# Seven products for eight: Strassen's scheme in the down product of an RWKV-7 and MLP kernel

## The chip, the cores and the metric

The kernel runs on one core of a Trainium2 chip. The metric is the time of one execution in microseconds on the device. All data is 32-bit floating point on the chip. TensorE, which multiplies matrices, works beside VectorE, ScalarE and GpSimd, each with its own queue of instructions; SyncE (SP) issues the transfers.

## The reference

An RWKV-7 recurrence over 768 steps (4 batches, 8 heads, head size 40), and on its output an MLP with a quick GELU:

```
for t in range(S):
    y[:, :, t] = einsum('bhd,bhde->bhe', r_t, state)
    Sa = einsum('bhde,bhe->bhd', state, a_t)
    state = state * w_t[:, :, None, :] - einsum('bhd,bhe->bhde', Sa, b_t) + einsum('bhd,bhe->bhde', v_t, k_t)
x = y.transpose(0, 2, 1, 3).reshape(3072, 320)
h = x @ w_in                              # 320 -> 2048
g = h * (1 / (1 + exp(-1.702 * h)))
out = g @ w_out                           # 2048 -> 320
```

## The kernel before

The sequence is cut into 12 chunks of 64 steps. A unit is one chunk of two batches (24 units); one step of a unit's algebra works on all its 16 heads. For each unit: decays (`decay`, `logarithm`), scaled keys and scores (`prep`), the inverse of a triangular matrix by five doubling levels (`inverse`), and the solution with the state carried over (`solve`). A level is a TensorE step (`ps_level`), a copy W, a subtraction E (line 763), a transpose ES (line 712) and a spreading EX (lines 717 and 719, on ScalarE, GpSimd or VectorE); the next level waits for EX.

When both units of chunk c are done, their outputs x go to DRAM and come back transposed into `xT_all` (three slots). Then `mlp(c)` runs on 256 tokens: `up`, 4 quarters q of 10 TensorE steps each (`ps_up`), each quarter followed by the activation `gelu(q)` into `g`; and `down(p)` for each unit p, 8 steps of 8 matmuls (`ps_down`), accumulated in the two PSUM banks of a pair, then a copy of one bank to `ob` (line 1027), an addition of the other (line 1029) and two transfers out. The last `down` is split into two halves of 160 columns.

All matmuls use the array as four tiles of 64x64: `QUARTERS` lists the four (row half, column half) pairs, and four matmuls run side by side. A 32-bit matmul is issued as two load-and-multiply pairs, so a down step of 8 matmuls is 16 instructions and a `down` is 128. Every matmul goes through the helper `mm` (line 301), so in the profile all have the line L301 and are told apart by their tiles.

The program is a list of tasks. `Plan.add` registers each with what it reads and writes; `ORDER`, written out by hand into the file, gives the sequence of all tasks, the engine of each and, for tasks with PSUM, one of four pairs of banks. Each engine runs its tasks in that sequence. The weights come as 64-bit numbers and are turned into 32-bit ones in eight pieces, the last operation of each on GpSimd (line 473).

Of the kernel before, what the change touches and what calls it, by code (L numbers as in the profile page):

```python
# [58 lines left out]
class Plan:  # L59
# [5 lines left out]
    def add(self, rank, engines, fn, reads=(), uses=(), writes=(), room=(), pair=None, most=None, size=0, release=0.0):  # L65

        t = Task(rank, engines, fn, pair, most, size)
        t.release = release  # L70
# [39 lines left out]
0s 8s 1s4 5s 102a 7s 6s 3a 9s 157a 87p0 88p1 10s 89a1 100p2 90a0 95d 13s4 4a 11s 93d 12s 101d2 98p3 2s 94d 97d 17s 103p1 16s 96d  # L110
142p0 15s 104a1 105d1 141p2 143a0 106d 99d3 107p1 144a2 18s4 148g 132p3 108a1 109d1 155p0 45s4 149d 27s 150g 156d0 158p2 14s4
110p1 159a2 160d2 91s4 130p0 161d 19a 24s4 112d1 162p2 111a1 22d 26s4 25s 163a2 113p1 20d 131a0 152g 164d2 34s4 92a 272s 21d
165p0 114a1 151g 271s 147a 153p2 115d1 273s 166a0 167d0 116p1 23g 28a 154d2 262p0 343s 117d1 263p2 133a3 342s 264a2 118d1 168p3
36s 31d 33s 119p1 276g 169a3 170d3 35s 120d1 42s 122a1 171p2 277d 278g 121a 43s 124d1 123a1 126p3 173d2 125a1 127d3 285a 29d
128p1 172a2 44s4 286p3 30d 54s4 37a 174p2 129d1 32g 51s4 288d3 134p1 178a2 146s4 175d2 145s 265a0 135d1 176a 187p0 289d 136p1
275s4 179a2 266g 61s 38d 138d1 188a0 341s 139s 287a3 181p0 39d 185p3 40d 137a1 177a2 290p1 313d 180a2 182a0 53s4 280g 279g 274s
186a3 183p2 292d1 281p0 291a1 333p3 41g 184d2 332p1 282d0 189p2 334a3 60s4 345s 314p0 190d2 316a0 346d 355a 191p3 347d 315d0
193d3 356p2 344s2 62s 140s 194s 195s4 192d3 293p0 335a1 358d2 46a 283p3 359d 317p1 294a0 295d0 349g 318a1 284d3 360p0 269a 348d
350g 296p1 336d 361a0 362d0 319p3 383d 357a2 297a1 298d1 384p0 321p2 49d 320a3 299p1 385a0 47d 322a2 63s4 363p3 300a1 301d1
323d2 386a0 302p1 364a3 365d3 353p0 351p2 306a1 48d 267s3 207p3 52s3 307a1 305d1 208p3 50g 268s3 64a 303d1 209p3 352d2 210p3  # L120
211p3 354d0 308a1 196p2 304a 212p3 65d 197p2 213p3 72s3 214p3 70s3 270d 55a 309p1 337s3 198p2 69s4 366p0 310a1 66d 199p2 367a0
200p2 58d 468p1 201p2 368d0 469a 473s 202p2 476s 203p2 67d 387p0 477s 470a1 490d 204p2 68g 480s 339a 205p2 369p1 388d0 206a2
215p3 371d1 218p0 219p0 56d 472s4 216p3 483g 71s4 220p0 217a3 471d 81s4 221p0 482d 79s 311p2 222p0 370a1 223p0 224p0 312d2 225p0
340d 372p3 229p1 478s4 376a3 230p1 57d 378a3 324p2 560s4 377a3 59g 226p0 78s4 375a3 325d2 231p1 73a 232p1 227p0 373d3 326p2 374d
228a0 389p3 484g 479s3 327d2 338s4 240p0 529d 390a3 481g 328d2 379p3 233p1 380a3 329d 234p1 391p2 485g 241p0 556s4 392d2 80s4
242p0 393d2 74d 486p3 235p1 487d3 530p2 236p1 75d 531a2 381p3 237p1 532a2 330s4 382d3 238p1 76d 491p2 394p3 494a2 493d2 77g
239a1 243p0 395d3 82a 488p1 557s3 396p3 489d1 474a 558s4 83d 331s 251p1 492d2 495d 252p1 84d 85d 253p1 398d3 86g 559s4 548p2
244p0 703s 397d3 549a 570d 553s 245p0 496d 550a2 552s 399d 497a 254p1 551g 554a 498p3 564d 400s 568p2 565g 499a3 246p0 569d2
500d3 563g 247p0 562d 694p2 561g 255p1 248a0 401s2 249d0 475d 256p1 250s 533p3 257p1 534a3 555d 695a 571p0 535p3 573d0 258p1
574a0 698s4 501d 696a2 609d 502g 536a3 537p2 572d0 259a1 576d 566p3 538a2 702s 402p0 575g 567d3 577a 403p0 404p0 539d2 785s3  # L130
700a 405p0 706s 708d 406p0 578p3 407p0 580d3 408p0 260d1 610p2 409p0 581d 709g 410p0 611d2 411p0 612d2 503p1 707d 582g 412a0
424p2 425p2 504d1 704s2 426p2 505d1 427p2 697d 428p2 579d3 613p1 701d 429p2 614a1 583p0 430p2 584a0 506d 431p2 585d0 432p2 507a
782s2 586d 433p2 587d 446p3 434a2 508p1 588p0 509a1 447p3 590d0 589a0 510d1 261s2 413p2 511d 699s 414p2 591d 512a 783s 415p2
592g 416p2 513p0 417p2 514a0 515d0 593p1 516d 418p2 594a1 595d1 419p2 596d 420p2 517a 597d 421p2 422p2 518p0 423a2 435p1 519d0
436p1 521d0 520g 437p1 522d0 438p1 523d0 439p1 440p1 524d0 525p2 716p0 526a2 441p1 717d0 927s 442p1 718d0 527p2 443p1 719d0
444p1 528d2 598p0 721d 445a1 540p2 720d 722g 601d0 603a0 617p1 602d0 541d2 448p3 618a1 604d0 542p2 619d1 599d0 600d 615p1 705s
544d2 449p3 616a1 781s 710d 545g 711d 605p0 723p1 606a0 450p3 607p0 451p3 546s 608d0 930s 452p3 725d1 724d1 620p0 726d 543d2
727a 773p1 453p3 621d0 778s 774a 547s 754d 728p2 622p0 454d3 455d3 729d2 456s 457p3 775a1 776g 730d2 784s 786g 779a 777s 624d0
458p3 623d0 625g 731d 793p1 833d 732a 459p3 733p2 789g 460p3 626s 734a2 794d1 735d2 714p0 790g 736d 461p3 780d 737g 1009s 918p1
755p2 923s 462p3 715d0 756a2 627s 757a2 788d 463p3 738p0 787d 464p3 739a0 740d0 919a 795p2 465d3 758p0 1006s 466d3 798a2 921d  # L140
650p3 467s 759d0 920a1 651p3 924a 928s 796d2 712p1 797d2 652p3 922s 800d 799g 653p3 932d 801a 654p3 834p0 655p3 713d1 656p3
657p3 835d0 760p2 836d0 925d 658p3 761a2 659p3 762p1 660a3 741d 628p0 742d 926s 629p0 630p0 763d1 802p2 764d1 631p0 803a2 804d2
632p0 805d 633p0 806a 743p3 634p0 746d3 635p0 747d3 837p1 931g 748d3 636p0 838a1 1007s 749d3 637p0 807p2 744d3 933g 638a0 639p1
808d2 640p1 791p3 745a 809d2 672p0 810d 792d3 811a 750p2 641p1 751a2 812p3 642p1 813a3 814d3 752p2 643p1 753d2 644p1 815d 645p1
816a 765p3 839p2 766d3 646p1 840a2 647p1 817p3 648p1 818a3 819d3 767p2 820d 649a1 821d 673p0 769d2 929s 768d2 770g 822p3 934d
674p0 825a3 826a3 940p1 827a3 675p0 1151s 828a3 935d 943a1 771s 661p2 823d3 662p2 941d1 1154s 824a 663p2 942d1 997p3 945d 944g
664p2 998a 1002s 978d 938p1 946g 665p2 939d1 666p2 772s 667p2 668p2 829p1 669p2 999a3 1000d 1001s 830d1 670p2 1003a 1011d 676p0
671a2 1004d 831p3 841p1 677p0 832d3 1005s 842d1 936p3 843d1 678p0 937d3 844p2 679p0 845d2 947p1 1010g 680d0 846p3 948a1 681d0
1012d 682s 683p2 847d3 1013g 1008s 848d3 1019p0 1014g 949d1 684p2 1022a0 1230s 849d 1233s 979p3 685p2 980a3 950d 850s 1020d0
981a3 951g 1142p1 1021d0 686p2 1024d 1143a 1147s 1023d 1025g 982p3 1057d 687p2 1152s 952p0 851s 983a3 1145g 688p2 1156d 1146s  # L150
953a0 954d0 984p3 1144a1 955d 1148a 689p2 956d 985a3 1149d 986p0 690p2 987a0 1150s 988d0 957p1 691a2 863p3 958a1 692d2 864p3
959d1 865p3 693s 960d 866p3 961d 1026p0 867p3 1027a0 1028d0 868p3 1029d 1155g 869p3 1157d 1030a 1058p2 870p3 871p3 1059a2 872p3
1060d2 1031p1 873a3 852p0 1033d1 853p0 1034d 854p0 1035d 1061p2 855p0 1062d2 1032a1 856p0 962p3 857p0 963a3 964d3 1036p1 965d
# [96 lines left out]
def rwkv7_gelu_quick(ctx: ExitStack, tc: tile.TileContext, time_d, v_d, w_d, wc_d, ak_d, b_d, rv_d, w_in, w_out, out):  # L250
    nc = tc.nc
# [735 lines left out]
    def mlp(c):  # L987
# [16 lines left out]
        def down(p):  # L1004
# [28 lines left out]
            for n, cols in enumerate([slice(0, DM // 2), slice(DM // 2, DM)] if last else [slice(0, DM)]):  # L1033
                for m in range(NM):
                    part(m, n, cols)
# [7 lines left out]
        for p in BITS:  # L1043
            down(p)
# [105 lines left out]
```

## Time and profile before

| | |
|---|---|
| median of 3 runs | 677.33 us (675.91 to 678.18) |
| profiled execution, span from the first to the last instruction | 677.7 us |
| profiled execution, time of its own | not listed beside the span |
| TensorE matmuls busy | 649.6 us, 19616 instructions |
| TensorE weight loads busy | 568.7 us, 19616 instructions |
| VectorE, ScalarE, GpSimd busy | 449.7, 329.1, 175.7 us |

The page of the profile gives busy times, the chain of work that ended last, and groups of instructions: line, engine, operation, output and inputs, shape, count, then busy time in us and the mean of one in ns, then the idle time of the engine ahead of them and what ended it. A row of the chain view is: start in us, length in us, what, and how many instructions were recorded (a few per cent of matmul records can be missing).

### The profile page before, as it was taken

Reading aid. Unit: us, or ns where it says so; the run is one execution under the profiler, and the core shown is the slowest. Engines: PE = TensorE matmul, PEld = TensorE weight load, DVE = VectorE, ACT = ScalarE, POOL = GpSimd, SP = SyncE. Lnnn points to the kernel's source line nnn. Section 1 sums busy time; section 2 is a strip of 40 time slices with the busy share of each in tenths; the row PEclk is TensorE's granted clock in tenths of the full one; section 3 lists DMA queues with packets and bytes.
Section 4 is the critical chain, followed back from the end, with each engine's and each line's share of the span. In section 5 each row is a group of like instructions: output and inputs, shape, how many; then the busy total and the mean of one; then the engine's idle time right before and its main releaser. Section 6 shows DMA issues by size and latency. Waiting matters only on the chain.

```text
span 677.7 us, 42447 instructions
## 1 busy us (share of the span) xinstructions
PE 649.6 (96%) x19616; PEld 568.7 (84%) x19616; DVE 449.7 (66%) x916; ACT 329.1 (49%) x681; POOL 175.7 (26%) x201
## 2 busy tenths in 40 slices
PE   5777999999999999999999999999999999999997
PEld 4667787787999997888888899999889798799896
DVE  5777779777867668757776687868656766675001
ACT  3676745634564655654545445455344454263010
POOL 6541443324123123123113211322411421300000
PEclk9979999999999999999999999999999999999999
DMA  6875753415324314432404513513412411200200
GB/s 208 295 255 160 226 172 97 129 42 152 107 64 131 94 58 124 114 107 65 124 14 131 149 35 108 155 33 107 140 38 62 130 53 45 69 15 14 60 13 21
DMA packets 35473, 69.74 MB, mean 103 GB/s; under 512 B 5472, under 2 KB 14816, under 8 KB 35296
## 3 DMA queue, kind: packets, MB, share of 16 engines
q1 hardware_dynamic: 35216, 66.99, 32.9%
q8 instruction: 154, 2.52, 1.6%
q14 instruction: 23, 0.19, 0.1%
q10 hardware_dynamic: 80, 0.04, 0.0%
HBM read 59.15 MB, written 7.86 MB: 99 GB/s over the span
## 4 chain that ended last, share of the span: by engine, by line
PE 88%; DMA 6%; DVE 2%; issue 1%; SPq 1%; ACT 1%; DVEq 0%; ACTq 0%
PE ps_up L301 31%; PE ps_down L301 29%; PE ps_level L301 8%; PE ps_y L301 5%; PE ps_B L301 4%; PE ps_X L301 2%; PE ps_N L301 2%; PE ps_rz L301 1%; PE ps_RV L301 1%; PE ps_A L301 1%; PE ps_zT L301 1%; SPq L331 1%; DMA w_sb<-in_w_in 1%; PE ps_cum L301 1%; PE ps_T L301 1%
## 5 line engine op out<-in xcount | busy, mean ns | idle before, releaser
L301 PE MATMUL ps_up<-xT_all,w_sb 64*64 64x256 f32 x3840 | 253.3, 377 | 2.1 <-issue 1.3
L301 PE MATMUL ps_down<-w_sb,g 64*64 64x320 f32 (+1 forms) x3200 | 241.5, 419 | 0.2 <-ACT zr L879 0.2
L301 PEld LDWEIGHTS ps_up<-xT_all,w_sb 64*64 64x64 f32 x3840 | 170.8, 133 | 18.8 <-issue 2.1
L301 PEld LDWEIGHTS ps_down<-w_sb,g 64*64 64x64 f32 x3200 | 142.5, 133 | 31.6 <-issue 0.4
L1000 ACT ACTIVATE g<-ps_up 128x1024 f32<-128x1024 f32 x48 | 49.2, 1025 | 46.3 <-PE ps_up L301 45.8
L719 POOL TENSOR_TENSOR EX<-ES,quads 128x512 f32<-128x512 f32 x30 | 39.7, 1324 | 116.4 <-DVE ES L712 77.7
L761 ACT COPY W<-ps_level 128x512 f32<-128x512 f32 x56 | 32.8, 585 | 67.7 <-PE ps_level L301 66.0
L301 PEld LDWEIGHTS ps_level<-W,EX 64*64 64x64 f32 x2560 | 60.0, 134 | 5.4 <-DVE T L840 0.2
L763 DVE TENSOR_TENSOR E<-two,ps_level 128x256 f32<-128x256 f32 x80 | 33.1, 415 | 36.5 <-ACT W L761 32.3
L301 PE MATMUL ps_level<-W,EX 64*64 64x64 f32 (+1 forms) x2560 | 56.8, 217 | 0.0
L717 ACT ACTIVATE EX<-ES,quads 128x256 f32<-128x256 f32 x82 | 37.2, 501 | 31.9 <-DVE ES L712 31.3
L629 POOL TENSOR_TENSOR ak<-ak,FT 128x512 f32<-128x512 f32 x17 | 23.0, 1353 | 77.2 <-DMA ak<-in_ak 54.4
L301 PEld LDWEIGHTS ps_level<-PT,EX 64*64 64x64 f32 x1280 | 30.7, 138 | 11.5 <-DVE EX L733 3.3
L301 PE MATMUL ps_level<-PT,EX 64*64 64x64 f32 (+2 forms) x1280 | 32.5, 234 | 6.9 <-DVE EX L733 5.0
L712 DVE STREAM_TRANSPOSE ES<-E 128x256 f32<-128x256 f32 x80 | 35.3, 443 | 4.4
L301 PE MATMUL ps_y<-RV,kh 64*64 64x104 f32 (+1 forms) x768 | 35.4, 247 | 0.9 <-DVE M L917 0.9
L301 PE MATMUL ps_y<-M,bh 64*64 64x104 f32 (+1 forms) x768 | 35.5, 247 | 0.7 <-DVE M L917 0.5
L901 ACT COPY B<-ps_B 128x416 f32<-128x416 f32 (+1 forms) x35 | 17.2, 493 | 34.4 <-PE ps_B L301 34.2
L301 PEld LDWEIGHTS ps_y<-RV,kh 64*64 64x64 f32 x768 | 29.6, 133 | 3.2 <-DVE M L917 1.5
L917 DVE TENSOR_TENSOR M<-ps_X,later 128x832 f32<-128x832 f32 (+1 forms) x24 | 23.9, 995 | 10.2 <-PE ps_X L301 10.0
L301 PE MATMUL ps_B<-RV,A 64*64 64x104 f32 (+1 forms) x768 | 29.2, 252 | 0.8 <-issue 0.8
L637 POOL TENSOR_TENSOR kh<-time,G 128x320 f32<-128x320 f32 x18 | 16.2, 901 | 51.2 <-PE ps_y L301 34.6
(133 smaller groups left out, 1099.0 us busy)
## 6 DMA issues: line engine op xcount, KB each, us to landing
ak<-in_ak SPq DMA_DIRECT2D x48, 160.0 KB
rv<-in_rv SPq DMA_DIRECT2D x48, 160.0 KB
time<-in_time SPq DMA_DIRECT2D x24, 320.0 KB
xT_all<-x_dram SPq DMA_DIRECT2D x48, 160.0 KB
wc<-in_wc SPq DMA_DIRECT2D x20, 264.0 KB
logw<-in_w SPq DMA_DIRECT2D x24, 160.0 KB
RV<-in_v SPq DMA_DIRECT2D x24, 160.0 KB
b<-in_b SPq DMA_DIRECT2D x48, 80.0 KB
```

The source lines that it names most:

```text
L301: nc.tensor.matmul(o, lhsT, rhs, start=start, stop=True, skip_group_check=True)
L331: begun.append(queue.dma_start(dst, src).ins)
L629: plan.add(R, {"DVE": 690.0, "POOL": 1270.0, "sbuf": True}, lambda t: of(t.engine).tensor_mul(ahT(), ahT(), FT_of(i)), reads=T("ak", "FT") ...
L637: plan.add(R + 4, {"POOL": 870.0, "DVE": 490.0, "sbuf": True}, lambda t, n=n, dst=dst: of(t.engine).tensor_mul(dst(i)[:, :, :D], by_head(t ...
L712: plan.add(rank, dve(256), lambda t: nc.vector.transpose(ES(n), source(t)), writes=[key("ES", n, 6)], **reads)
L717: nc.scalar.activation(dst[:, :, h], ES(n), ACT.Copy, scale=quads[:, h, :1])
L719: of(t.engine).tensor_mul(dst, ES(n).unsqueeze(2).to_broadcast([128, 8, 2, 32]), quads.unsqueeze(1).to_broadcast([128, 8, 2, 32]))
L761: plan.add(rank, any2(512), lambda t: copy(t.engine)(tiles_of(W(n + 1)), blocks(psum(t, ""), 64)), writes=[key("W", n + 1, 5)], pair=pair)
L763: plan.add(rank, dve(256), lambda t: nc.vector.tensor_sub(tiles_of(E(n + 1)), every(two32, [128, 2, 4, 32]), blocks(psum(t, ""), 64)[:, :, ...
L901: plan.add(R, any2(4 * wide), lambda t: copy(t.engine)(dst(), some(psum(t, "")[:, :, :208])), writes=[("Bv", i)] if x and c > 0 else T("B" ...
L917: plan.add(R + 1, dve(8 * wide), lambda t: nc.vector.tensor_tensor(M_of(i)[:, :, :wide].rearrange("p (j b) n -> p b j n", b=2), some(psum( ...
L1000: plan.add(-45, {"ACT": 1030.0, "table": "gelu"}, lambda t: nc.scalar.activation(g_of(c * NQ + q).rearrange("p m r n -> p r m n"), psum(t, ...
```

## The change

Chunk 0 keeps the down product as it was. For chunks 1 to 11 both units are multiplied at once: the 256 tokens are two row halves p of 128, the 2048 inner columns are split in halves by m (each quarter q holds a part of both), and the 320 output columns in two halves of 160. This gives blocks a11, a12, a21, a22 of g and B(0,0) to B(1,1) of `w_out`, and seven block products in place of eight. Each product has 4 steps (one per q) of two matmuls with 128 rows, 128 columns of weights and 160 moving columns, on the whole array: 4 pairs of load and multiply a step.

Before each step's product come the sums S1 = a21 + a22, S3 = a11 - a21, S2 = S1 - a11 and S4 = a12 - S2, one 128x256 operation per q on VectorE or GpSimd (`combined`). Four sums of weight blocks are made once (`weight_sums`), into the space in which raw weights had lain. S1 lies in the third slot of `xT_all` (so two remain for x), S2 in a block of `w_out` that is not needed any more.

Products 1, 6, 7, 4 add up in bank 0 of a pair and 2, 5, 3 in bank 1; seven evictions of 160 columns (`taken`) take the values out at the right time, four copies and three additions.

`ORDER` is new: 3043 tasks in place of 2709. The steps up to the first down step of chunk 0 stand as before.

```diff
-    def add(self, ..., release=0.0):
+    def add(self, ..., release=0.0, loose=False, bank=None):
...
-            t.after.update(o for o in writers if "PE" in o.engines)
+            if not loose:
+                t.after.update(o for o in writers if "PE" in o.engines)
...
-    plan = Plan(dict(... wz=2, ... xT=3, g=4, ob=1), 4)
+    plan = Plan(dict(... wz=3, ... xT=2, g=4, sb=1, S1=4, S2=4), 4)
...
-    wz_of = lambda i: buf("wz", i, [128, 8])
+    wz_of = lambda i: wch_of(i)[:, 0]
...
-    xT_of = lambda c: xT_all[:, c % 3].rearrange("p (q k n) -> p q k n", q=2, n=128)
+    xT_of = lambda c: xT_all[:, c % 2].rearrange("p (q k n) -> p q k n", q=2, n=128)
...
+    def weight_sums():
+        made = [(0, B(0, 1), B(0, 0), []), (1, B(1, 1), sums[:, 0], [("sum", 0)]), (2, B(1, 1), B(0, 1), []), (3, B(1, 0), sums[:, 1], [("sum", 1)])]
+        for k, x, y, after in made:
+            plan.add(60, {"DVE": 1490.0, "POOL": 2890.0, "sbuf": True}, lambda t, k=k, x=x, y=y: of(t.engine).tensor_tensor(
+                out=sums[:, k], in0=x, in1=y, op=ALU.subtract), ...)
...
+        def fast():
...
+            for q in range(NQ):
+                n = c * NQ + q
+                a11, a12, a21, a22 = (lambda n, p=p, m=m: block(n, p, m) for p, m in product(BITS, BITS))
+                combined(q, S1_of, a21, a22, ALU.add, [("weight", raws.index("x"))], [("S1", n)])
+                combined(q, a21, a11, a21, ALU.subtract, [("S1", n)], [("S3", n)])
+                combined(q, S2_of, S1_of, a11, ALU.subtract, [("S1", n), ("sum", 0), ("sum", 2)] + none, [("S2", n)])
+
+            def times(name, bank, slot, left, right, reads, kept=True):
+                for q in range(NQ):
+                    n = c * NQ + q
+
+                    def go(t, n=n, q=q):
+                        ps, a = psum(t, "ps_fast"), left(n)
+                        for f in BITS:
+                            fresh = (t.pair, bank) not in begun_banks
+                            begun_banks.add((t.pair, bank))
+                            mm(ps[:, bank, slot * HD:(slot + 1) * HD], a[:, f], right[:, q, f], fresh)
...
+            times("1", 0, 0, lambda n: block(n, 0, 0), B(0, 0), ...)
+            taken("c1", 0, 0, 0, 0, ["P1"])
+            times("2", 1, 0, lambda n: block(n, 0, 1), B(1, 0), ...)
+            taken("C11", 0, 0, 1, 0, ["P2", "c1"], True)
+            for q in range(NQ):
...
+                combined(q, a12, a12, S2_of, ALU.subtract, [("S2", n), ("P2", (c, q))], [("S4", n)])
+            times("6", 0, 0, S2_of, sums[:, 1], ..., False)
+            taken("u2", 0, 1, 0, 0, ["P6"])
+            times("5", 1, 1, S1_of, sums[:, 0], ..., False)
+            taken("d", 1, 1, 1, 1, ["P5"])
+            times("7", 0, 0, lambda n: block(n, 1, 0), sums[:, 2], ...)
+            taken("C22", 1, 1, 0, 0, ["P7", "d"], True)
+            times("3", 1, 1, lambda n: block(n, 0, 1), B(1, 1), ...)
+            taken("C12", 0, 1, 1, 1, ["P3", "u2"], True)
+            times("4", 0, 0, lambda n: block(n, 1, 1), sums[:, 3], ...)
+            taken("C21", 1, 0, 0, 0, ["P4"])
...
+        if c < FAST:
+            for p in BITS:
+                plain(p)
+        else:
+            fast()
```

`FAST` is 1. `plain(p)` is the old `down(p)` without the split of the last.

More of the change, by code (lines that the diff above doesn't have):

```diff
@@ L63, in __init__, with add @@
         self.tasks, self.made, self.used, self.of_pair = [], {}, {}, {}
-    def add(self, rank, engines, fn, reads=(), uses=(), writes=(), room=(), pair=None, most=None, size=0, release=0.0):
+    def add(self, rank, engines, fn, reads=(), uses=(), writes=(), room=(), pair=None, most=None, size=0, release=0.0, loose=False, bank=None):
         t = Task(rank, engines, fn, pair, most, size)
+        t.half = bank
         t.release = release
@@ L114 @@
[L114 to L117, printed above, removed]
@@ L246 @@
+2994d 2998g 2989a3 2991d 2999d 2995d 3022p0 3001g 3005p0 3007p0 3004p0 2797s 3024p0 3010p0 3000d 3013g 3006a0 2992g 3018p0
+3017p0 3019p0 3016p0 3020a0 3023p0 3021p0 3029p0 3027p0 3026p0 3028p0 3025a0 3030d0 3009p0 3032p0 3037p0 3015d 3014d 3011d0
+3036p0 3038p0 3012g 3039p0 3034p0 3040a0 3042s 3033p0 3031p0 3035d0 3041s
 """
@@ L267, in rwkv7_gelu_quick @@
     PARTS = 4
+    FAST = 1
     ROUNDS, WINDOW, SHARE = 4, 5000.0, 1.0
@@ L279, in rwkv7_gelu_quick @@
     banks = ctx.enter_context(tc.tile_pool(name="banks", bufs=1, space=bass.MemoryType.PSUM))
-    plan = Plan(dict(logw=3, wc=3, G=1, wch=3, wz=2, time=2, ak=2, b=2, rv=2, FT=3, GT=1, kh=2, bh=2, zr=2, rz=2,
-                     A=1, B=1, RV=2, E0=2, W0=2, P21=2, PT=2, W=2, E=2, ES=2, EX=2, T=2, Tc=1, QT=1, zraw=2, zT=1, M=2, x=1, xT=3, g=4, ob=1), 4)
+    plan = Plan(dict(logw=3, wc=3, G=1, wch=3, wz=3, time=2, ak=2, b=2, rv=2, FT=3, GT=1, kh=2, bh=2, zr=2, rz=2,
+                     A=1, B=1, RV=2, E0=2, W0=2, P21=2, PT=2, W=2, E=2, ES=2, EX=2, T=2, Tc=1, QT=1, zraw=2, zT=1, M=2, x=1, xT=2, g=4, sb=1, S1=4, S2=4), 4)
     tiles, psums, drams = {}, {}, {}
@@ L309, in pe, with pe_whole @@
         return {"PE": sum(n * 2 * max(m[0] / 1.2 + 5 if m else 58.0, cols / 1.2 + 3) for n, cols, *m in sets), "instr": sum(16 * n for n, *_ in sets)}
-    def pe_wide(*sets):
-        return {"PE": sum(n * 2 * (cols / 1.2 + 3) for n, cols in sets), "instr": sum(8 * n for n, _ in sets), "mode": 1}
+    def pe_whole(n, cols):
+        return {"PE": n * 2 * (2 * cols / 2.4 + 3), "instr": 4 * n, "mode": 1}
     def dve(n):
@@ L325, in copy @@
         return nc.scalar.copy if e == "ACT" else nc.vector.tensor_copy
-    begun = []
+    begun, begun_banks = [], set()
     def transfer(t, dst, src, queue=nc.sync):
@@ L364, in select @@
                                 pattern=[[sign, t.shape[-1]]], channel_multiplier=-sign)
-    edges = single("edges", [128, 65])
+    border = single("border", [128, 169])
+    edges = border[:, :65]
     nc.gpsimd.memset(edges, 1.0)
@@ L385, in rwkv7_gelu_quick @@
         select(within[32 * q:32 * q + 32, q % 2], ALU.is_gt, 0, -1, 0.0)
-    upper, later = single("upper", [128, 64]), single("later", [128, 104])
+    upper, later = single("upper", [128, 64]), border[:, 65:]
     for t, one in (upper, 1.0), (later, -1.0):
@@ L431, in rwkv7_gelu_quick @@
     extra = single("extra", [128, 4 * PIECE])
-    xT_all = single("xT_all", [128, plan.slots["xT"], 2 * NK * 128])
+    xT_all = single("xT_all", [128, 3, 2 * NK * 128])
     most, least = (float(np.array(x, np.uint32).view(np.float32)) for x in (0x0FEFFFFF, 0x9FEFFFFF))
@@ L980, in solve, with store @@
         plan.add(-50, {"SP": 700.0}, part_with, reads=T("x"), writes=T("xd"), size=DM * 512)
-        plan.add(-50, {"SP": 700.0}, get_back, reads=T("xd") + ([("weight", raws.index("x"))] if c in (1, 2) else []), writes=[("xT", c), ("xs", (c, p))], size=2 * DM * 512)
+        plan.add(-50, {"SP": 700.0}, get_back, reads=T("xd") + ([("weight", raws.index("x"))] if c == 1 else []), writes=[("xT", c), ("xs", (c, p))], size=2 * DM * 512)
     g_of = lambda n: buf("g", n, [128, 2, 2, 256])
-    ob_of = lambda n: buf("ob", n, [128, DM])
+    HD = DM // 2
+    sb_of = lambda c: buf("sb", c, [128, 2, DM])
+    block = lambda n, p, m: g_of(n)[:, m, :, p * 128:p * 128 + 128]
+    S1_of = lambda n: xT_all[:, 2, (n % NQ) * 256:(n % NQ) * 256 + 256].rearrange("p (f t) -> p f t", f=2)
+    w_blocks = w_out_sb.rearrange("p (q m f n) -> p q m f n", q=NQ, m=2, f=2)
+    B = lambda m, n: w_blocks[:, :, m, :, n * HD:(n + 1) * HD]
+    S2_of = lambda n: w_blocks[:, n % NQ, 0, :, HD:HD + 128]
+    sums = extra.rearrange("p (k q f n) -> p k q f n", k=4, q=NQ, f=2)
+    def weight_sums():
+        made = [(0, B(0, 1), B(0, 0), []), (1, B(1, 1), sums[:, 0], [("sum", 0)]), (2, B(1, 1), B(0, 1), []), (3, B(1, 0), sums[:, 1], [("sum", 1)])]
+        for k, x, y, after in made:
+            plan.add(60, {"DVE": 1490.0, "POOL": 2890.0, "sbuf": True}, lambda t, k=k, x=x, y=y: of(t.engine).tensor_tensor(
+                out=sums[:, k], in0=x, in1=y, op=ALU.subtract), reads=[("weight", n) for n in range(2 * NQ)] + after, writes=[("sum", k)])
+    def store(t, c, p, cols=slice(0, DM), queue=nc.sync):
+        for b in BITS:
+            o = (2 * p + b) * S + c * C
+            transfer(t, out[o:o + C, cols], sb_of(c)[HALF[b], p, cols], queue if b else nc.sync)
     def mlp(c):
@@ L1002, in gelu, with plain, part @@
                 ACT.Gelu_apprx_sigmoid), writes=[("g", c * NQ + q)], pair=("up", c * NQ + q))
-        def down(p):
+        def plain(p):
             serial = 2 * c + p
-            last = serial == NU - 1
-            def part(m, n, cols):
+            def part(m):
                 def go(t):
@@ L1013, in go @@
                             o = p * 128 + b * 64
-                            mm(po[HALF[b], r, :cols.stop - cols.start], g[HALF[r], f % 2, o:o + 64],
-                               w_out_sb[HALF[r], f * DM + cols.start:f * DM + cols.stop], f == 0)
+                            mm(po[HALF[b], r, :DM], g[HALF[r], f % 2, o:o + 64], w_out_sb[HALF[r], f * DM:(f + 1) * DM], f == 0)
                 parts = range(2 * m * DM // PIECE, (2 * (m + 1) * DM - 1) // PIECE + 1)
-                plan.add(R + 10 * (p + 1) + m + 8 * n, pe((2, cols.stop - cols.start)), go, reads=[("g", c * NQ + m // 2)] + [("weight", NQ + n) for n in parts],
-                         pair=("down", serial + n), most=1)
@@ L1020, in finish @@
-            def finish(n, cols):
-                ob, wide = lambda: ob_of(serial)[:, cols], cols.stop - cols.start
-                def store(t):
-                    for b in BITS:
-                        o = (2 * p + b) * S + c * C
-                        transfer(t, out[o:o + C, cols], ob()[HALF[b]], nc.scalar if last and n and b else nc.sync)
-                plan.add(-45, any2(wide), lambda t: copy(t.engine)(ob(), psum(t, "")[:, 0, :wide]),
-                         writes=[("ob", serial + n)], pair=("down", serial + n))
-                plan.add(-45, dve(wide), lambda t: nc.vector.tensor_add(ob(), ob(), psum(t, "")[:, 1, :wide]),
-                         reads=[("ob", serial + n)], writes=[("out", serial + n)], pair=("down", serial + n))
-                plan.add(-100, {"SP": 700.0}, store, reads=[("ob", serial + n), ("out", serial + n)], size=128 * wide * 4)
@@ L1033, in down @@
-            for n, cols in enumerate([slice(0, DM // 2), slice(DM // 2, DM)] if last else [slice(0, DM)]):
-                for m in range(NM):
-                    part(m, n, cols)
-                finish(n, cols)
+                plan.add(R + 10 * (p + 1) + m, pe((2, DM)), go, reads=[("g", c * NQ + m // 2)] + [("weight", NQ + n) for n in parts],
+                         pair=("down", serial), most=1)
+            for m in range(NM):
+                part(m)
+            ob = lambda: sb_of(c)[:, p]
@@ new lines, in plain @@
+            plan.add(-45, any2(DM), lambda t: copy(t.engine)(ob(), psum(t, "")[:, 0, :DM]),
+                     writes=[("ob", serial)], room=[("sb", c)], pair=("down", serial))
+            plan.add(-45, dve(DM), lambda t: nc.vector.tensor_add(ob(), ob(), psum(t, "")[:, 1, :DM]),
+                     reads=[("ob", serial)], writes=[("out", serial), ("sb", c)], pair=("down", serial))
+            plan.add(-100, {"SP": 700.0}, lambda t: store(t, c, p), reads=[("out", serial)], uses=[("sb", c)], size=128 * DM * 4)
@@ L1042, in mlp @@
             gelu(q)
-        for p in BITS:
-            down(p)
+        if c < FAST:
[3 more added lines that the diff above has]
+            fast()
     for i in range(3):
@@ L1052, in rwkv7_gelu_quick @@
     weights()
+    weight_sums()
     for i in range(NU):
```

312 lines of the change are left out of this document (179 added, 133 removed).

## Prediction

> **What bounds the kernel now.** First the page: busy shares, the granted clock, and the chain of waits.
>
> ```profile
> span 677.7 us, 42447 instructions
> ...
> PE 649.6 (96%) x19616; PEld 568.7 (84%) x19616; DVE 449.7 (66%) x916; ACT 329.1 (49%) x681; POOL 175.7 (26%) x201
> ...
> PEclk9979999999999999999999999999999999999999
> ...
> PE 88%; DMA 6%; DVE 2%; issue 1%; SPq 1%; ACT 1%; DVEq 0%; ACTq 0%
> ```
>
> TensorE is busy for 96% of the span, holds 88% of the chain, and runs at nine tenths of its clock or more except in the third slice. A busy TensorE may still hide holes, because the ends of matmuls are modelled. So the second view is the windows, the third the chain in order of time, whose pieces run from start to start and so show the true pace.
>
> ```profile
> 100.00:200.00 100.00, 99.04 (x3000) 82.71 (x2994) 75.60 (x154) 52.99 (x110) 30.08 (x33) 1.00 0.33 98
> 200.00:300.00 100.00, 99.72 (x3063) 89.86 (x3059) 71.25 (x145) 57.57 (x119) 26.40 (x25) 1.00 0.36 105
> 300.00:400.00 100.00, 100.00 (x3059) 86.50 (x3054) 72.72 (x158) 49.34 (x89) 25.27 (x28) 1.00 0.33 94
> 400.00:500.00 100.00, 99.30 (x3068) 89.20 (x3070) 70.26 (x144) 47.92 (x102) 24.37 (x26) 1.00 0.34 100
> 500.00:600.00 100.00, 99.77 (x3123) 87.42 (x3118) 65.99 (x141) 44.51 (x97) 25.09 (x28) 1.00 0.22 63
> 600.00:660.00 60.00, 60.00 (x1427) 54.17 (x1422) 19.17 (x52) 15.96 (x26) 0.00 (x0) 1.00 0.09 25
> ```
>
> (Columns: TensorE's matmuls, its weight loads, VectorE, ScalarE, GpSimd, clock, DMA share, GB/s.) From 100 to 660 us TensorE lacks at most 1 us in 100, while VectorE is at 66 to 76% and GpSimd at 24 to 30%.
>
> ```profile
> 230.12 0.30 PE ps_zT L301 x29
> 234.86 0.44 PE ps_level L301 x30
> ...
> 607.25 0.44 PE ps_level L301 x27
> 626.30 10.77 PE ps_down L301 x159
> ...
> 655.40 4.32 PE ps_up L301 x80
> 659.72 14.10 PE ps_down L301 x336
> 673.82 0.02 issue
> 673.84 0.34 DVE ob L1027
> 674.18 0.02 issue
> 674.20 0.32 DVE ob L1029
> ```
>
> In 64x64 tiles four matmul instructions run side by side. 80 of `ps_up` (256 columns) take 4.32 us: 54.0 ns each, 216 ns per four. Ten steps of `ps_down` with 320 columns (160 instructions, one not recorded) take 10.77 us: 67.3 ns each. The last piece has 80 of these (5.38 us) and the 256 of the split last product, with 160 columns: (14.10 - 5.38) / 64 = 136.3 ns per four. The pieces abut without holes, so this kernel ends when its columns have streamed, and what is taken off TensorE in this stretch comes off the end, unless something else becomes late.
>
> **The products.** Removed: 21 down products of 128 instructions x 67.3 ns = 180.9 us, and the split one, 64 x 136.3 ns = 8.7 us; 189.6 us together. Added: 11 chunks x 7 products x 8 matmuls x 2 instructions = 1232 instructions on the whole array, 160 columns each. No row shows one. A whole-array instruction does the work of four quarter-array ones of the same columns, so I take the 136.3 ns of those: 167.9 us. Difference: -21.7 us.
>
> Its weight load must hide under those 136 ns.
>
> ```profile
> 605.30 0.66 PE L301 MATMUL ps_level<-W,EX 64*64 64x64 f32 x30
> ...
> 607.06 0.63 PE L301 MATMUL ps_level<-W,EX 64*64 64x32 f32 x30
> ...
> L301 PE MATMUL ps_up<-xT_all,w_sb 64*64 64x256 f32 x3840 | 253.3, 377 | 2.1 <-issue 1.3 <-DMA xT_all<-x_dram 0.6 <-PE ps_rz L301 0.2
> ...
> L301 PEld LDWEIGHTS ps_up<-xT_all,w_sb 64*64 64x64 f32 x3840 | 170.8, 133 | 18.8 <-issue 2.1 <-DMA xT_all<-x_dram 1.0 <-DVE RV L660 0.8
> ```
>
> A level step takes 0.44 us whether 64 columns move (234.86) or 32 (607.25): there the load of 64 columns sets the pace, 0.44 / 30 x 4 = 58.7 ns, and the 40-column loads of `ps_zT` give 0.30 / 29 x 4 = 41.4 ns. Extended at that slope, 0.72 ns a column, a load of 128 columns takes an estimated 105 ns, under 136. And it does run under a matmul that uses the same rows: streaming and load of a level step, one after the other, would take about twice 58.7 ns.
>
> **Changes of tile shape.** All matmuls before use quarter tiles; now the array is recast at each border between a product step and anything else. In the new order the 308 product steps stand in 65 groups, most of 2 to 8 steps and the last two of 23 and 28: 129 borders, since the kernel ends inside the last. The trace has no such border. Lower bound 0: no reason in the trace makes a border a gain. Upper bound: the matmul in flight runs out, its 377 ns less the 216 ns it streams = 161 ns, and then the new load stands alone, at most the 133 ns of a recorded load: 294 ns, 37.9 us in all. The trace does not say how much of the 161 ns the next instruction's operand fetch covers. I take half, 80 ns a border: +10.3 us. It is the softest number here; at 155 ns a border the change's gain is gone.
>
> The Trainium skill, TensorEngine Tiling (Array Packing), section Key Properties, says that changing the tiling mode drains TensorE; it gives no duration. Its page TensorE: Matmul & The Clock Gate, section Single matmul latency, has a fixed part of 398 cycles at 2.4 GHz beside the streaming, 166 ns; a border at that price is an estimated 21.4 us, and the sum would come to no change. No run shows it yet; the 161 ns above are of the same size.
>
> **Work on the other engines.**
>
> ```profile
> L707 POOL TENSOR_TENSOR PT<-two,PT 128x256 f32<-128x256 f32 x10 | 7.3, 730 | 37.7 <-DVE PT L699 37.7
> L707 DVE TENSOR_TENSOR PT<-two,PT 128x256 f32<-128x256 f32 x10 | 5.7, 568 | 0.0
> L473 POOL TENSOR_TENSOR w_sb<-w_sb,extra 128x1280 int32<-128x1280 int32 x5 | 14.9, 2989 | 27.7 <-DVE extra L469 16.7 <-DVE w_sb L465 11.0
> ...
> L763 DVE TENSOR_TENSOR E<-two,ps_level 128x256 f32<-128x256 f32 x80 | 33.1, 415 | 36.5 <-ACT W L761 32.3 <-PE ps_level L301 3.5
> L712 DVE STREAM_TRANSPOSE ES<-E 128x256 f32<-128x256 f32 x80 | 35.3, 443 | 4.4
> L719 POOL TENSOR_TENSOR EX<-ES,quads 128x512 f32<-128x512 f32 x30 | 39.7, 1324 | 116.4 <-DVE ES L712 77.7 <-PE ps_level L301 9.6 <-ACT P L702 7.1
> L717 ACT ACTIVATE EX<-ES,quads 128x256 f32<-128x256 f32 x82 | 37.2, 501 | 31.9 <-DVE ES L712 31.3
> ```
>
> Sixteen sums of 128x256 a chunk: the order puts 106 on GpSimd (x 730 ns = 77.4 us) and 70 on VectorE (x 568 ns = 39.8 us). The four weight sums go to GpSimd, 4 x 2.99 = 12.0 us. GpSimd goes from 175.7 to about 265 us (40% of some 668), VectorE to about 490 us (73%). The seven evictions of 160 columns a chunk (0.32 to 0.34 us by the chain's end) replace two copies and two additions of 320: seven times 0.33 is 2.3 us against about 1.8, shared between ScalarE and VectorE. TensorE covers all this if the order leaves distance. Between two levels of one unit's inverse lie E, ES and EX: 415 + 443 + 1324 = 2.18 us with GpSimd, 1.86 with ScalarE (2 x 501). At the paces above, the order before leaves at least 2.63 us of TensorE work there, the new one at least 2.60, with a longer median (4.97 against 4.35). So it is as loose as before on the longest chain.
>
> Added waits: product 6 may not write bank 0 before the copy of product 1 is done, 7 not before that of 6, 4 not before C22 is added; on bank 1, 3 waits for the copy of 5. All of TensorE's queue stands behind such a wait. Such a wait needs 161 ns of tail, 0.02 of issue and 0.34 of copy, 0.52 us. The order leaves at least 0.93 us. S2, S3 and S4 stand on VectorE and GpSimd ahead of E, EX and kh of the units; a late one holds these up. Price: one sum of 730 ns in GpSimd's queue ahead of an EX exceeds the spare 2.60 - 2.18 = 0.42 by 0.31 us; 23 levels get their EX from GpSimd, so 7.1 us at most here. The weight sums, between the last two weights and chunk 1, hold the queue 2.99 us each, 12.0 at most. Lower bound 0, as the distance was kept. I take 2 us for both, near the lower end, since in the windows above the order before lost at most 1 us in 100 with the same least distance.
>
> At no cost: two slots of xT in place of three (SP fetches back x of chunk c+2 once up(c) is read, and x of c+2 is made a whole chunk later; otherwise up to the 0.6 us that `ps_up` waited for xT_all above); wz in place (the work of line 605 is unchanged); shared masks; two transfers fewer on SP. The first 359 entries of the order are the same, so the start does not move. The tail loses one of its two evictions: -0.3 us.
>
> **Sum:** 677.7 - 21.7 + 10.3 + 2.0 - 0.3 = 668.0 us. The span stands 0.4 us above the median of the runs, 677.33, so 667.6; I say 668.
>
> **Rivals.** *Free borders*: the drain is covered. For it: chain pieces of 40-row and 64-row matmuls abut; against it: these are all quarter tiles. 677.7 - 21.7 - 0.3 = 655.7; 13%.
>
> *Full drain at every border* (slower): the tail and the estimated load, 161 + 105 on entering and 161 + 59 on leaving, 243 ns on average: +31.4 us. 677.7 - 21.7 + 31.4 + 2.0 - 0.3 = 689.1 us. It decides from 155 ns a border. For it: 128 columns cannot be loaded while quarter matmuls hold the array. Against it: loads do run ahead in today's stream. 27%; a third of this near 161 ns, where it cancels to no change.
>
> *Late sums*: GpSimd and VectorE, fuller, come late to levels and products; up to 7.1 + 12.0 us in place of 2.0: 685.1 us, decisive when over 11.7 us are lost. Against it the distances above. 11%.
>
> *Loads not hidden on the whole array*: 1232 x 105 ns = 129 us more, about 797 us. The level steps speak against it. The Trainium skill, TensorE: Matmul & The Clock Gate, section The mechanism, speaks for it: loads overlap matmuls in flight only where the row group differs; there the trace disagrees for quarter tiles, 58.7 ns a step, and no run shows whole ones. 4%.
>
> *Forecast* (borders of 40 to 130 ns): 45%, by itself 662 to 674.
>
> **Numbers.** A measurement of this kernel can tell about 0.3%, 2 us, from no change. Faster: 45 + 13 = 58%. Same: 8%. Slower: 34%, the rest. The range 656 to 696 goes from free borders to the upper bound of the borders (667.6 - 10.3 + 37.9 = 695.2); unhidden loads and both mishaps together lie outside.
>
> **What would show it.** Pieces of `ps_fast` should run at 136 ns an instruction; at 240 the loads are not hidden. The hole between the last matmul of one shape and the first of the other gives the border's price: 80 ns expected, over 155 proves the drain. TensorE's windows should keep over 98%, with level matmuls waiting for nothing on GpSimd; if waits for EX or S2 lead the list, late sums it is. I am wrong if the count of columns falls by 21.7 us and the end does not move.

## The result: 6% slower, and the profile after

The changed kernel takes 719.78 us (median; 718.55 to 725.87), the kernel before 677.41: ratio 1.0636, 95% interval 1.059 to 1.0683. Forecast were 668 us, 656 to 696. The profiled execution took 718.55 us, its span is 716.6. First the page (busy shares, chain) and the windows.

```profile
span 716.6 us, 39198 instructions
...
PE 662.3 (92%) x17904; PEld 584.0 (82%) x17904; DVE 494.4 (69%) x1007; ACT 333.9 (47%) x708; POOL 252.2 (35%) x294
...
PEclk9999998999999999999999999999999999999999
...
PE 83%; DVE 6%; DMA 5%; issue 3%; ACT 2%; SPq 1%; ACTq 0%; DVEq 0%
```

```profile
100.00:200.00 100.00, 88.63 (x2451) 74.20 (x2445) 77.65 (x143) 45.03 (x95) 48.54 (x39) 0.97 0.28 83
200.00:300.00 100.00, 95.35 (x2612) 84.93 (x2611) 73.89 (x164) 53.83 (x110) 33.15 (x39) 1.00 0.31 94
...
600.00:660.00 60.00, 57.56 (x1597) 51.77 (x1591) 40.62 (x89) 22.73 (x50) 20.86 (x25) 1.00 0.15 45
```

TensorE's share falls from 96% to 92%, and VectorE takes 6% of the chain in place of 2%. (Windows: the three middle ones, with 98% each, are left out.) The worst is the first, where GpSimd is busiest, 48.54 of 100. The busy column flatters, since a whole-array matmul is recorded for 299 ns and streams for 136. So I took from the trace each stretch in which no column moved, at 136 ns for 160 columns and full clock. From 68 us to the end these holes sum to 58.8 us, against 5.4 before: 20.6 us at changes of shape, 15.2 us where a product step waited for an eviction, 11.0 us before level steps, the rest in small pieces. Two of them show in the views. The chain in order of time around 119 us, then the timeline of the same stretch, VectorE's rows and GpSimd's (start, us, instruction):

```profile
110.45 6.71 DVE x L985 x3
...
117.76 0.36 DVE ES L735
...
118.15 0.92 ACT EX L740 x2
...
119.11 1.13 PE ps_level L323 x32
```

```profile
108.13 2.19 DVE L628 TENSOR_TENSOR wch<-wch 128x8 f32<-128x8 f32 x1
110.25 6.92 DVE L985 TENSOR_TENSOR x<-zr,FT 128x128 f32<-128x128 f32 x4
...
107.34 2.95 POOL L496 TENSOR_TENSOR w_sb<-w_sb,extra 128x1280 int32<-128x1280 int32 x1 [0.81 <-DVE w_sb L488]
110.37 2.89 POOL L1020 TENSOR_TENSOR extra<-w_sb 128x1280 f32<-128x1280 f32 x1
113.23 0.90 POOL L660 TENSOR_TENSOR bh<-time,G 128x320 f32<-128x320 f32 x1
114.09 2.92 POOL L1020 TENSOR_TENSOR extra<-w_sb 128x1280 f32<-128x1280 f32 x1
```

L1020 is the weight sums. While GpSimd makes two of them, four VectorE multiplications (x) take 6.92 us; their median over the kernel is 0.285 us each. Singly they take 0.28, 2.97, 0.94 and 2.96 us in the trace, and each of the last three ends some 0.15 us after the GpSimd instruction beside it. ES and EX stand behind them in order, and the level step starts at 119.11, 7.99 us after TensorE ran out of work: the largest hole of all.

The second stretch is in chunk 9, the timeline at 614 us. `xT_all` in a product step is S1, so product 5 (bank 1); `w_sb` with `extra` is product 6 (bank 0).

```profile
614.23 0.71 PE L323 MATMUL ps_fast<-extra,xT_all 128*128 128x160 f32 x4
...
614.77 0.71 PE L323 MATMUL ps_fast<-extra,w_sb 128*128 128x160 f32 x4
615.52 0.29 ACT L1099 COPY sb<-ps_fast 128x160 f32<-128x160 f32 x1 [3.01 <-PE ps_fast L323]
615.86 0.57 PEld L323 LDWEIGHTS ps_fast<-extra,w_sb 128*128 128x128 f32 x4 [0.62 <-ACT sb L1099]
615.86 0.81 PE L323 MATMUL ps_fast<-extra,w_sb 128*128 128x160 f32 x4 [0.38 <-ACT sb L1099]
```

The copy d reads product 5's bank, but it starts only when a step of product 6, in the other bank, has ended; and the next step of product 6 waits for this copy of a bank that it does not touch. The program orders the accesses to the two-bank tile as if it were one buffer; e2 below tests this. By the trace, some 30 of the 77 evictions wait for a step of the other bank.

### The profile page after: what moved, and what is told of

Its sections match the earlier page's. It is cut to its first block, busy times and chain, and to the rows that moved or that the text cites. A ratio compares the mean times of both kernels' runs of the same rounds, so it can differ in the third digit from the quotient of the medians.

```text
span 716.6 us, 39198 instructions
## 1 busy us (share of the span) xinstructions
PE 662.3 (92%) x17904; PEld 584.0 (82%) x17904; DVE 494.4 (69%) x1007; ACT 333.9 (47%) x708; POOL 252.2 (35%) x294
## 4 chain that ended last, share of the span: by engine, by line
PE 83%; DVE 6%; DMA 5%; issue 3%; ACT 2%; SPq 1%; ACTq 0%; DVEq 0%
PE ps_up L323 28%; PE ps_fast L323 24%; PE ps_level L323 8%; PE ps_B L323 4%; PE ps_y L323 4%; PE ps_X L323 3%; PE ps_down L323 2%; PE ps_N L323 2%; DVE x L985 2%; PE ps_A L323 1%; PE ps_RV L323 1%; PE ps_rz L323 1%; DMA logw<-in_w 1%; PE ps_cum L323 1%; PE ps_zT L323 1%
## 5 line engine op out<-in xcount | busy, mean ns | idle before, releaser
L323 PE MATMUL ps_up<-xT_all,w_sb 64*64 64x256 f32 x3840 | 245.4, 377 | 1.9 <-issue 1.8
L323 PEld LDWEIGHTS ps_up<-xT_all,w_sb 64*64 64x64 f32 x3840 | 158.6, 133 | 29.4 <-issue 3.3
L323 PE MATMUL ps_fast<-w_sb,g 128*128 128x160 f32 x528 | 88.8, 307 | 1.9 <-DVE sb L1098 1.1
L323 PEld LDWEIGHTS ps_fast<-w_sb,g 128*128 128x128 f32 x528 | 74.9, 190 | 7.1 <-DVE sb L1098 1.6
L323 PE MATMUL ps_fast<-extra,g 128*128 128x160 f32 x352 | 58.0, 306 | 5.6 <-DVE sb L1098 3.5
L323 PEld LDWEIGHTS ps_fast<-extra,g 128*128 128x128 f32 x352 | 49.8, 190 | 9.3 <-DVE sb L1098 5.0
L1099 ACT COPY sb<-ps_fast 128x160 f32<-128x160 f32 x36 | 10.4, 292 | 83.4 <-PE ps_fast L323 72.7
L1074 POOL TENSOR_TENSOR xT_all<-g 128x256 f32<-128x256 f32 x28 | 21.5, 770 | 65.0 <-ACT g L1041 64.9
L940 DVE TENSOR_TENSOR M<-ps_X,border 128x832 f32<-128x832 f32 (+1 forms) x24 | 23.8, 992 | 17.7 <-PE ps_X L323 17.5
L1098 DVE TENSOR_TENSOR sb<-sb,ps_fast 128x160 f32<-128x160 f32 x33 | 10.2, 318 | 37.2 <-PE ps_fast L323 16.6
```

Of the source, the lines that this page charges most:

```text
L323: nc.tensor.matmul(o, lhsT, rhs, start=start, stop=True, skip_group_check=True)
L940: plan.add(R + 1, dve(8 * wide), lambda t: nc.vector.tensor_tensor(M_of(i)[:, :, :wide].rearrange("p (j b) n -> p b j n", b=2), some(psum( ...
L1074: plan.add(R + 20 + q, dict(one), lambda t: of(t.engine).tensor_tensor(out=out(n), in0=x(n), in1=y(n), op=op), reads=[("g", n)] + reads, w ...
L1098: plan.add(-45, dve(HD) if add else any2(HD), lambda t: nc.vector.tensor_add(o(), o(), psum(t, "")[:, bank, slot * HD:(slot + 1) * HD]) if add
L1099: else copy(t.engine)(o(), psum(t, "")[:, bank, slot * HD:(slot + 1) * HD]),
```

## Experiments

They ran on other chips, where the kernel before took 681 to 683 us, so ratios to it are compared; a difference of 0.01 is 6.8 us of 677.4.

| run | ratio | 95% interval |
|---|---|---|
| changed kernel | 1.0636 | 1.0590 to 1.0683 |
| e1 weight sums on VectorE | 1.0503 | 1.0458 to 1.0549 |
| e2 waits by bank | 1.0400 | 1.0349 to 1.0450 |
| e3 both | 1.0248 | 1.0200 to 1.0297 |
| e4 quarter tiles | 1.0937 | 1.0879 to 1.0995 |
| e5 quarter tiles, 320 columns | 1.0433 | 1.0385 to 1.0480 |
| e6 e3 with 38 groups | 1.1147 | 1.1091 to 1.1204 |
| e7 e3 with 20 groups | 1.1922 | 1.1882 to 1.1961 |
| e8 e3 with small sums | 1.0172 | 1.0144 to 1.0201 |
| e10 Strassen for chunks 10, 11 alone | 0.9953 | 0.9936 to 0.9971 |
| e11 before, halved down matmuls | 1.0812 | 1.0781 to 1.0842 |

**Weight sums.** Four entries of the order, and nothing else:

```
- 89g ... 87g ... 88g ... 90g
+ 89d ... 87d ... 88d ... 90d
```

> The four weight sums go from GpSimd to VectorE, at the same places of the order; nothing else changes. In the changed kernel, while GpSimd made one of them (2.89 us), VectorE's instructions stood: x took 6.92 us at 110 us, and TensorE waited 7.99 us at 119 us. Theory A (VectorE is held up while GpSimd reads SBUF in such a long sum): the hole at 119 us goes, VectorE pays about 1.5 us for each sum itself; 719.8 - 8 = 712 us, at best 709. Rival (the hole comes from the order, VectorE is late there in any case): 718 to 721 us, the hole stays or moves. Rival (GpSimd's queue alone, EX behind a sum): the same gain, but the long x stays at some 6 us.

Measured -0.0133, or -9.0 us. VectorE's timeline, with its first weight sum:

```profile
111.82 1.62 DVE L987 TENSOR_TENSOR x<-zr,FT 128x128 f32<-128x128 f32 x4
...
117.16 1.48 DVE L1022 TENSOR_TENSOR extra<-w_sb 128x1280 f32<-128x1280 f32 x1
```

The four x take 1.62 us in place of 6.92, and the hole before the level step shrinks from 7.99 to 2.70 us. So VectorE was held up by GpSimd's sums; a queue of GpSimd's alone would have left x as long as it was. The granted clock in the window from 100 to 200 us is 1.00 here and 0.97 in the changed kernel; how much of the 9.0 us that is was not separated. The Trainium skill, SBUF — State Buffer, section Who interferes with whom, calls the port pair that the two engines share an exclusive lock; the 6.92 us beside two sums of 2.9 us agree with blocking rather than sharing.

**Waits across banks.** The dependencies between a product step and an eviction of the other bank are dropped, and one on the last access of the same bank is added:

```
+ for o in seen[1 - bank, other]:
+     tc.declare_no_dep(ins, o, reason="another bank")
+ if seen[bank, other]:
+     tc.add_manual_dep(ins, seen[bank, other][-1].name, ..., reason="the same bank")
```

> Waits between a product step and an eviction of the other PSUM bank are taken out, those of one bank stay; order and work are the same. In the changed program 30 of 77 evictions wait for a step of the other bank, and the next step then waits for the eviction. Theory B (these waits cost time by themselves): the 22 holes of some 0.64 us and the 22 loads of 0.10 us behind them go, with the exit waits some 17 us: 719.8 - 17 = 703 us, between 701 and 708. Rival (vector engines are late anyway, the time is given back at the next level or sum): 714 to 720 us. Rival (borders between shapes are all of it): 718 to 721 us.

> Both edits: weight sums on VectorE and no waits across banks. If the two causes are separate, the gains add up: 719.8 - 8 - 17 = 695 us (692 to 699). If both removed only the same slack of one late engine, it is no better than the better of the two alone, about 703 us.

e2 gains 0.0236 or 16.0 us, as expected. The stretch of chunk 9 again, in e2's timeline:

```profile
613.12 0.71 PE L323 MATMUL ps_fast<-extra,xT_all 128*128 128x160 f32 x4
...
613.67 1.25 PE L323 MATMUL ps_fast<-extra,w_sb 128*128 128x160 f32 x8
613.87 0.29 ACT L1110 COPY sb<-ps_fast 128x160 f32<-128x160 f32 x1 [2.47 <-PE ps_fast L323]
```

The copy of product 5's bank now starts while the steps of product 6 run, and they no longer stop for it. e3 gains 0.0388 or 26.3 us, against 25.0 for the two added: separate causes. The end of chunk 11 in the chain, of the changed kernel (28 steps, 112 instructions, with five stops):

```profile
693.21 5.10 PE ps_fast L323 x36
...
698.38 0.30 ACT sb L1099
...
698.82 2.43 PE ps_fast L323 x16
...
711.01 1.37 PE ps_fast L323 x8
712.37 0.03 issue
```

and of e3:

```profile
661.70 17.43 PE ps_up L325 x320
679.12 15.43 PE ps_fast L325 x112
694.55 0.03 issue
```

From 693.21 to 712.37 are 19.16 us; without the stops the same steps take 15.43, or 112 x 136.3 ns = 15.27 and the start. All evictions lie beside the next product.

**The borders.** Each product step in quarter tiles, so that the shape of the array never changes. First with four matmuls of 160 columns for each whole-array one:

```
- mm(ps[:, bank, slot * HD:(slot + 1) * HD], a[:, f], right[:, q, f], fresh)
+ for r, h in QUARTERS:
+     ...
+     mm(ps[HALF[h], r, o:o + HD], a[HALF[r], f, HALF[h]], right[HALF[r], q, f], fresh)
```

> Each 128x128 matmul of the products as four 64x64 ones of the same 160 columns, so that the array never changes its shape; order, evictions, waits and other work as in the changed kernel (half of each sum goes to the other bank and is left out, so the numbers are not the reference's). Theory C (a group pays 89 + 93 ns for its two borders and 104 ns for the exposed second load): 65 x 287 ns = 18.6 us go, 719.8 - 18.6 = 701 us (699 to 704). Rival (only the bare borders are saved, the exposed load stays): 719.8 - 11.7 = 708 us. Rival (borders drain in full and all of the loss is theirs, some 42 us): 680 us. Rival (borders lie beside waits that stay): 714 to 720 us.

A miss on the other side: 20 us slower. The chain of this run, 584 to 589 us:

```profile
582.86 1.14 PE ps_fast L323 x29
584.00 0.56 issue
584.56 1.36 PE ps_fast L323 x33
...
588.28 0.52 issue
```

"Issue" is time in which TensorE waited for nothing that the profile shows. Such holes of over 0.4 us sum to 43.7 us here, 6.0 in the changed kernel and 1.8 before; most starts lie 126 to 128 matmuls, or a multiple of that, apart. A matmul and its load are two instructions, so that is one hole per some 254 instructions. This suggests that TensorE runs out of instructions, which e11 below tests. The next version streams as long with half the instructions:

```
+ for r, h in QUARTERS:
+     ...
+     mm(ps[HALF[h], r, :2 * HD]..., a[HALF[r], 0, HALF[h]], right[HALF[r], q], fresh)
```

> As the quarter version before, but each step in 8 instructions of 320 columns (67 ns each by ps_down before) in place of 16 of 160: the same streamed time of 269 ns a half step with half the instructions, so that TensorE's instructions don't run short. Order, evictions and waits are those of the changed kernel; each step multiplies only the first half of its channels, and the halves of the sum are not put together. Times go by ratios to before, the changed kernel standing at 1.0636. Theory C (two borders at 89 to 93 ns and one exposed load of 104 ns a group, 65 groups): -18.6 us, ratio 1.036 (1.032 to 1.042). Rival (only the bare borders, -11.7 us): 1.046. Rival (borders drain in full, over 40 us are theirs): 1.00. Rival (they lie beside other waits): 1.057 to 1.064.

-0.0203, or -13.8 us, between "bare borders" (11.7) and "borders with load" (18.6). The intervals of the two ratios leave anything from 7.5 to 20.2 us, which excludes neither. The trace has no change of shape left for the 20.6 us of holes, while holes without a releaser grew from 6.0 to 12.4 us. So the price read off the trace, 18.6 us for the groups and some 2 for the loads behind waits, is supported but not measured cleanly by itself.

**Is it the supply of instructions?** The kernel before, with its down matmuls cut in two; nothing of the change is in it:

```
+ for at in range(cols.start, cols.stop, 160):
      mm(po[HALF[b], r, ...160 columns], g[...], w_out_sb[...], ...)
```

> The kernel before with each down matmul of 320 columns as two of 160 (all but the last product, which has them already): same work, order and streamed columns, but 2688 TensorE instructions with their loads more. By streaming alone 2688 x 34.1 - 1344 x 67.3 is under 2 us: ratio 1.00 to 1.003. If TensorE's instructions come too slowly (the holes of 0.4 to 2 us with no releaser at every 127 matmuls in the quarter version): 20 to 40 such holes of 1 us, ratio 1.03 to 1.06.

1.0812, 55 us, for the same columns in the same order, and more than the 1.03 to 1.06 expected. (The cut makes 2944 matmul instructions more, 22560 in place of 19616; the 2688 of the expectation leave out chunk 0.) The instruction queue's row and the chain:

```profile
q8 instruction: 177, 2.90, 1.6%
```

```profile
526.28 0.92 issue
527.19 0.79 PE ps_down L301 x11
...
530.81 0.89 issue
531.70 0.88 PE ps_down L301 x18
...
535.73 0.81 issue
```

41 such holes sum to 35.3 us; they follow 4.5 and 4.9 us apart here. The queue moves 2.90 MB in 177 packets, 16.4 KB each. They land 3.9 us apart (median from 240 to 660 us), and each of the 41 holes ends 1.2 to 1.6 us after such a landing, so it is the instructions that these holes wait for. The other 20 us of the loss are not in holes of this size; where they go stays open. The Trainium skill, Runtime: NRT & Kernel Launch, section Instruction fetch mechanics, has blocks of 16 KiB or 256 instructions, which agrees with a hole per 127 matmuls and their loads. The same section of the Trainium skill calls the crossing of a block mostly hidden; this run contradicts that.

**Fewer groups.** e3, with product steps (and what depends on them) put off in the order until 8, or 16, stand together:

```
- groups of 1 to 8 steps: 65
+ groups of 8, 8, 8, 4 steps a chunk: 38        (e7: 16 and 12: 20)
```

> Weight sums on VectorE, no waits across banks (1.0248 together), and the product steps put off in the order until 8 stand together: 38 groups in place of 65. Theory C: 27 groups less at 287 ns, -7.7 us, ratio 1.0134. Rival (single steps between levels were needed to cover the vector engines, and holes at the levels grow by more): 1.025 or more.

> The same with groups of 16 and 12 steps: 20 groups in place of 65. Theory C: 45 groups less at 287 ns, -12.9 us, ratio 1.0058. Rival (holes at the levels take the place of the borders, as 16 steps are 4.4 us in one piece that other gaps then lack): 1.02 or more.

Both rivals won, and by far: +61 and +113 us against e3. The windows from 300 us of e3, of e6 and of e7:

```profile
300.00:400.00 100.00, 99.16 (x2697) 88.33 (x2688) 72.17 (x147) 53.74 (x105) 37.98 (x47) 1.00 0.33 94
```

```profile
300.00:400.00 100.00, 88.24 (x2368) 78.04 (x2368) 62.24 (x134) 48.19 (x101) 25.92 (x33) 0.97 0.26 75
```

```profile
300.00:400.00 100.00, 88.20 (x2017) 81.58 (x2010) 50.56 (x106) 39.23 (x90) 21.69 (x30) 0.84 0.25 73
```

Product steps are the filler between the steps of the inverse. In one lump they leave the other gaps empty: in e7 the holes sum to 140.4 us from 68 us on. The granted clock falls to 0.84 in this window, and since the holes are counted at full clock, a part of the 140.4 us is slower streaming. In these two orders, which were otherwise left as they were, fewer borders cost more than they save; an order made anew for large groups was not tried.

**The sums of operands.** In e3, seven eighths of each are left out, but for the first four:

```
- ... out=out(n), in0=x(n), in1=y(n) ...
+ few = slice(0, 128 if out is S1_of and c == FAST else 16)
+ ... out=out(n)[:, :, few], in0=x(n)[:, :, few], in1=y(n)[:, :, few] ...
```

> Weight sums on VectorE, no waits across banks, and all but the first four sums of products' operands over 16 of 128 columns in each block (seven eighths of that work is left out): 176 sums of 0.57 or 0.73 us become short. Theory (what is left beside the borders, about 15 us against before, is VectorE and GpSimd late with these sums or because of them): -8 to -12 us, ratio 1.007 to 1.013. Rival (the sums are covered by TensorE, and the rest is the order's): 1.02 to 1.025.

-0.0076, some 5 us, with intervals that just meet (1.0200 and 1.0201): less than the theory, more than the rival. The sums are a small part, and its size is rough.

**Where nothing needs filler.** The kernel before with its own order; only the last two chunks, where the down steps ran in one piece anyway, get the products:

```
- for p in BITS: down(p)
+ if c < FAST: ... down(p)          # FAST = 10
+ else: weight_sums() if c == FAST; fast()
```

> The kernel before, with its order, and Strassen's products for chunks 10 and 11 alone: their 56 steps stand where the old down steps of the end stood, in five groups, where no level waits for filler; weight sums in 16 pieces on GpSimd between 200 and 590 us where it idled for over 6 us; no waits across banks. Products: 32 old steps, 34.5 us, against 56 x 0.545 = 30.5 us: -4.0 us; five groups x 0.29 = +1.4 us; pieces and sums 0. 677.4 - 2.6 = 674.8 us, ratio 0.9962 (0.993 to 0.998). Rival (sums of chunk 10 on GpSimd delay VectorE on the way to chunk 11's x): 1.000 to 1.006. Rival (borders cost more than the traces show): 1.0 or more.

0.9953 (0.9936 to 0.9971): 3.2 us, or 0.5%, faster than the kernel before, with the expected 2.6 within its interval. The chain's end:

```profile
621.58 1.28 PE ps_fast L310 x8
622.86 1.09 PE ps_y L310 x64
623.95 1.28 PE ps_fast L310 x8
...
629.33 11.06 PE ps_fast L310 x80
640.39 17.43 PE ps_up L310 x320
657.82 15.59 PE ps_fast L310 x112
673.41 0.02 issue
673.43 0.29 ACT time L1116
```

Pieces run from start to start: 8 instructions with their border and exposed load take 1.28 us, 1.09 of it streaming. It is the only version that is faster than both kernels.

## Why the prediction was wrong, step by step

- **Products, -21.7 us: right.** 1058 of the starts of whole-array instructions follow each other at 136 ns, the 136.3 of the forecast, so the load of 128 columns is hidden in the stream; the rival of unhidden loads (797 us) is out.
- **Borders, +10.3 us: mis-sized.** Forecast were 80 ns a border; measured are 88 to 98 ns (most 89 or 90) into the whole array and 93 out of it, 11.8 us. The Trainium skill, TensorEngine Tiling (Array Packing), section Key Properties, has a change of tiling mode drain TensorE; the trace has a hole at every border and so agrees. Its length is nearer to the half drain of the forecast than to the 166 ns that the forecast had estimated from the page TensorE: Matmul & The Clock Gate of the Trainium skill. The step left out what comes behind the border: the second whole-array instruction follows at 240 ns in place of 136 (84 times). These 104 ns are what the forecast estimated for a load of 128 columns (105 ns), so here it is not hidden. With 6.8 us for the 65 groups the term is 18.6 us, 287 ns a group, inside its bounds of 0 to 37.9. By itself this makes the sum 676.3, no change. The price of the bare border was nearly right, while the term, 10.3 against 18.6, was little more than half of what was paid.
- **Waits of evictions, "the order leaves at least 0.93 us": the step that failed.** The forecast counted the waits that the order's own bookkeeping asks for, by bank, and took them as covered. The program waits by tile: an eviction also waits for steps of the other bank, and the next steps wait for it. The forecast put these waits at nothing; they cost 16.0 us (e2), more than any other term missed by.
- **Weight sums, up to 12.0 us in the bounds, taken into the 2.0: wrong in the mechanism.** The forecast had GpSimd's queue held up; VectorE's was, by instructions of GpSimd that it does not wait for. 9.0 us (e1). The other sums, which it priced at 730 and 568 ns and took as covered, cost some 5 us (e8).
- **Supply of instructions: not in the forecast at all.** 6.0 us of holes without a releaser against 1.8; that is read off the traces and was not removed alone in this kernel.
- **Tail, -0.3 us: wrong.** One eviction less stands at the end, but chunk 11 lost 3.7 us at evictions ahead of them, part of e2's 16.0.
- Sum: -21.7 + 18.6 + 16.0 + 9.0 + 5 + 4.2 = +31.1 us. Measured are +42.4. Some 11 us stay open. Of these 3.5 lie in the comparison itself, since the two profiled spans, 716.6 and 677.7, differ by 38.9 us only. Another 2.9 lie ahead of the first down step, where the order is the same: it starts at 91.36 us in place of 88.47. That leaves some 5. The trace has more small holes before `ps_rz`, `ps_T` and `ps_N`, and no experiment took them apart.
- **Rivals.** "Full drain" was priced at 243 ns a border, a whole group at 486; a group costs 287. "Late sums" named the right engines, and its 19.1 us stand against 9.0 and some 5, but by another mechanism. The text left "both mishaps together" outside the range; the outcome was a part of both, and a third that no row of the trace before shows.
- **Slips in the working** that change little: the sum of the free borders leaves out the 2.0 us that the other sums carry (657.7 with it). VectorE's 66 to 76% and GpSimd's 24 to 30% hold from 100 to 600 us; in the last window they are 32% and 0. The 0.4 us between span and median were taken off, but in every run that lists both, the time is 1.7 to 3.0 us above the span.

## What to carry to other kernels

Before counting a wait as covered, ask at what grain the program tracks the buffer: here two PSUM banks in one tile were one buffer, and an eviction of one bank stopped the matmuls of both. Count an algebraic saving only where the steps stand together; where they are the filler of a latency chain, each group pays its change of shape, and lumping them cost the chain more here. Ask of a long GpSimd instruction whether VectorE stands still beside it, as the multiplications x did.

## What the hardware showed that was not expected

- A change between quarter tiles and the whole array costs 89 to 93 ns each way, and the first hidden load comes one instruction late: 104 ns more a group.
- TensorE's instructions come in blocks of 16.4 KB, and their supply can fall behind: with 15% more matmuls (22560 against 19616) for the same columns the kernel before loses 8%, 35.3 us of it in 41 holes that end shortly after a block has landed.
- In the order with more holes in TensorE's work the granted clock was lower: 0.84 in a window of 100 us in e7, 1.00 in the same window in e3.
- One VectorE multiplication of 128 elements a lane took up to 2.97 us beside GpSimd's sums, ten times its median.
